# Linear attention and a routed expert network on one core: another order of work in a unit, the decay check beside the experts, one zero product a unit

## The chip, the cores and the metric

The kernel runs on one NeuronCore of a Trainium2 chip. Its engines are TensorE (PE in the rows; PEld is its weight load), VectorE (DVE), ScalarE (ACT), GpSimd (POOL) and SyncE (SP), which here only issues DMAs. Each engine works through its own instructions in order and waits on semaphores for the others. The metric is the device time of one execution in microseconds (us). Beside it stands one profiled execution, whose trace gives the start and the duration of every instruction.

## What is computed

Three stages, cut from the reference:

```python
for t in range(S):                       # gated linear attention, S=768, D=48, 4 batches x 8 heads
    state = alpha[:, :, t, :, None] * state + k[:, :, t] (x) v[:, :, t]
    y[:, :, t] = q[:, :, t] @ state
x = y as (3072 tokens, 384)
e = argmax(x @ w_gate)                   # one of 8 experts a token, gate g from the softmax
x = g * (relu(x @ w1[e]) @ w2[e])        # 384 -> 1024 -> 384
h = relu(x @ w_in)                       # 384 -> 2048
out = (h * h) @ w_out                    # 2048 -> 384
```

## The kernel before

*Units.* The attention is cut into 32 units: a unit is two heads of one batch and one half of the sequence, that is three chunks of 128 steps. Units 0 to 15 are the first halves, 16 to 31 the second halves, which begin from the state `smid` that the first half left. Channels of a unit lie on 112 partitions (48, a gap, 48). What is loaded for a unit is `qka`: q, k and alpha, 505 KB, in one of six buffers.

*A unit's work.* `scan` (L185, VectorE) gives A, the running product of alpha in each chunk. `prep_a` (L192 to L194, ScalarE) takes R = exp(-ln A), and in a third operation the decay check: Relu(alpha - 1), summed into `chk`, which shall be zero (`junk` is thrown away). `prep_p` (L203, L204) makes M = R k and R = A R on GpSimd, for the first two units on VectorE. `prep_k` and `prep_q` (L209, L214, VectorE) make `kk` = (2 - R) M and `qq` = q A. TensorE then takes `scores` = kk'qq into the bank `sct` (L229), `masked` (L236, VectorE) multiplies with the causal mask into `pt`, `ktr` (L245) transposes kk, and ScalarE copies it to `kn` (L246). `state_pe` (L256) makes the chunks' updates of the state in the bank `pst`; `state_0` to `state_4` carry the state over the chunks, with adds T on VectorE (L265) and multiplications by A on ScalarE (L261) in turn. `yout` (L293, L297) adds pt'v and S'qq into the bank `py`, ScalarE copies it to `yt`; `xout` (L316) multiplies with the identity and w_gate, which brings tokens on partitions and gives the logits, in `px`; ScalarE copies x (L318), VectorE adds the logits (L325, L327). All these buffers are rings of two to six.

*Zero products and warm-ups.* `fill` (L220) multiplies zeros into the bank that is to be overwritten, once ahead of the scores and once ahead of `yout` in every unit; `warm` (L102) does so ahead of the first units. They compute nothing.

*Routing.* Each four units make a group of tokens complete. `route_a` (seven operations on VectorE, L351 to L361), `route_b` (two products) and `route_s` (two operations) give each token its slot, and `scatter` (GpSimd's DMA, L388) writes the tokens to the slots in HBM. After unit 28 the first part of expert 0's tokens is loaded back (`xload(0)`, L404), and behind the loop it is transposed (L442) and the experts begin.

*Order.* All is in `tc.manual_schedule()`: the order of the calls in the code is the order on every engine. The loop's body handles several units at once: in pass u it works on the scores of u+1, the output of u and the logits of u-1, and prepares units further ahead. SP issues the loads in the same order and stops at each whose buffer isn't free.

*Experts.* For expert e a step f of eight does nine products of the first layer for 128 hidden channels (`gemm1`, L457, into the banks `pk` and `st` in turn), ScalarE's Relu (L470) and VectorE's remainder (L471), and nine products of the second layer for the step two before (L487). Beside it run the splits of the next weights into high and low parts (ScalarE L124, VectorE L125), the loads of weights (`wload`, L111, half an expert in a buffer of a ring of two), and the conversion of the last layers' weights from 64 bits (`conv`, L722 to L747, on SP, GpSimd, VectorE, ScalarE). The last stage (L778 to L830) does the same for the last network. `check` and `check_flag` sum `chk` and other conditions into a flag; where it isn't met, a general path runs, which isn't entered for this data.

## Time and profile before

| | us |
|---|---|
| median of three runs | 830.01 (829.81 to 835.50) |
| profiled execution, its own time | 824.76 |
| its span, first to last instruction | 822.8 |
| TensorE busy | 808.0 (98%) |
| VectorE busy | 554.6 (67%) |
| ScalarE busy | 394.7 (48%) |
| GpSimd busy | 273.7 (33%) |

The sums of busy time are means over stages that differ: the scan stage ends at some 164 us, the experts follow to some 420 us, then the last network. Idle time of an engine that is waited for by nobody costs nothing, so each stage is read by what ends its waits. Start-to-start distances say more of TensorE than durations do, since its products overlap.

### The profile page before, as it was taken

Reading aid. Unit: us, or ns where it says so; the run is one execution under the profiler, and the core shown is the slowest. Engines: PE = TensorE matmul, PEld = TensorE weight load, DVE = VectorE, ACT = ScalarE, POOL = GpSimd, SP = SyncE. Lnnn points to the kernel's source line nnn. Section 1 sums busy time; section 2 is a strip of 40 time slices with the busy share of each in tenths; the row PEclk is TensorE's granted clock in tenths of the full one; section 3 lists DMA queues with packets and bytes.
Section 4 is the critical chain, followed back from the end, with each engine's and each line's share of the span. In section 5 each row is a group of like instructions: output and inputs, shape, how many; then the busy total and the mean of one; then the engine's idle time right before and its main releaser. Section 6 shows DMA issues by size and latency. Waiting matters only on the chain.

```text
span 822.8 us, 14398 instructions
## 1 busy us (share of the span) xinstructions
PE 808.0 (98%) x5348; PEld 725.0 (88%) x5348; DVE 554.6 (67%) x1086; ACT 394.7 (48%) x885; POOL 273.7 (33%) x310
## 2 busy tenths in 40 slices
PE   8999999999999999999999999999999999999996
PEld 4777777799999999999989999988999999999996
DVE  6788988658588897865547878887464444344352
ACT  4777777545444545444344444444463233333342
POOL 2446766320165565510006566562000101011021
PEclk9899999999999999999999999999999999999999
DMA  9896892265767676754222443622412032021111
GB/s 270 267 293 195 256 270 81 54 222 159 246 197 215 221 248 186 228 199 136 72 86 83 114 142 105 212 61 68 154 60 96 19 97 82 35 96 58 40 59 62
DMA packets 56990, 118.12 MB, mean 144 GB/s; under 512 B 12272, under 2 KB 36688, under 8 KB 54608
## 3 DMA queue, kind: packets, MB, share of 16 engines
q1 hardware_dynamic: 52144, 100.59, 40.1%
q0 software_dynamic: 3072, 9.55, 3.1%
q10 hardware_dynamic: 1696, 6.98, 2.7%
q8 instruction: 44, 0.72, 0.4%
q14 instruction: 34, 0.28, 0.1%
HBM read 85.38 MB, written 31.73 MB: 142 GB/s over the span
## 4 chain that ended last, share of the span: by engine, by line
PE 88%; DVE 7%; issue 2%; ACT 2%; DMA 0%; POOL 0%; POOLq 0%; DVEq 0%; ACTq 0%
PE ph L457 38%; PE bp L797 10%; PE pair L487 10%; PE bpx L797 7%; PE bpy L797 7%; PE third L487 5%; PE sct L229 2%; PE px L316 2%; DVE pt L236 2%; PE py L293 2%; PE py L297 1%; DVE A L185 1%; PE pk L245 1%; PE sct L220 1%; PE pst L256 1%
## 5 line engine op out<-in xcount | busy, mean ns | idle before, releaser
L780 DVE TENSOR_TENSOR room<-room 128x512 f32<-128x512 f32 (+1 forms) x112 | 77.7, 694 | 147.3 <-ACT room L778 147.2
L778 ACT ACTIVATE room<-ph 128x512 f32<-128x512 f32 (+1 forms) x112 | 60.2, 538 | 235.8 <-PE ph L457 235.7
L457 PE MATMUL ph<-xth,w00h 128*128 128x512 f32 (+3 forms) x288 | 102.1, 354 | 0.0
L457 PE MATMUL ph<-xth,w00l 128*128 128x512 f32 (+3 forms) x288 | 100.8, 350 | 0.0
L457 PE MATMUL ph<-xtl,w00h 128*128 128x512 f32 (+3 forms) x288 | 100.2, 348 | 0.0
L830 POOL DMA_INDIRECT out<-room,id x24 | 23.6, 983 | 228.5 <-DVE room L813 223.3
L457 PE MATMUL ph<-xth,w10h 128*128 128x512 f32 (+2 forms) x264 | 95.6, 362 | 0.0
L457 PE MATMUL ph<-xtl,w10h 128*128 128x512 f32 (+2 forms) x264 | 95.4, 361 | 0.0
L457 PE MATMUL ph<-xth,w10l 128*128 128x512 f32 (+2 forms) x264 | 95.3, 361 | 0.0
L781 DVE TENSOR_TENSOR htl<-room,hth 128x512 fp32r<-128x512 f32 (+1 forms) x112 | 74.5, 665 | 15.2 <-ACT cvg L743 0.5
L727 POOL TENSOR_TENSOR cvg<-cvg,cvd 128x256 f32<-128x256 f32 x48 | 39.8, 829 | 120.5 <-issue 78.2
L732 POOL TENSOR_SCALAR cvc<-cvt 128x256 f32<-128x256 f32 x48 | 38.0, 792 | 103.1 <-DMA cvt<-wf 64.4
L470 ACT ACTIVATE hth<-ph 128x448 fp32r<-128x448 f32 (+2 forms) x72 | 36.2, 503 | 61.6 <-PE ph L457 59.4
L779 ACT ACTIVATE hth<-room 128x512 fp32r<-128x512 f32 (+1 forms) x112 | 63.9, 571 | 3.6
L471 DVE SCALAR_TENSOR_TENSOR htl<-ph,hth 128x448 fp32r<-128x448 f32 (+2 forms) x72 | 40.9, 568 | 30.1 <-ACT hth L470 29.6
L457 PEld LDWEIGHTS ph<-xtl,w00h 128*128 128x128 f32 x288 | 54.2, 188 | 6.7 <-DVE xtl L435 0.2
L457 PEld LDWEIGHTS ph<-xth,w00h 128*128 128x128 f32 x288 | 54.4, 189 | 5.1
L457 PEld LDWEIGHTS ph<-xth,w00l 128*128 128x128 f32 x288 | 54.2, 188 | 4.3
L457 PEld LDWEIGHTS ph<-xtl,w10h 128*128 128x128 f32 x264 | 49.5, 188 | 5.9
L457 PEld LDWEIGHTS ph<-xth,w10h 128*128 128x128 f32 x264 | 49.6, 188 | 4.6
L457 PEld LDWEIGHTS ph<-xth,w10l 128*128 128x128 f32 x264 | 49.6, 188 | 4.4
L203 POOL TENSOR_TENSOR M<-R,qka 112x384 f32<-112x384 f32 x30 | 29.9, 998 | 61.6 <-DVE pt L236 41.9
(218 smaller groups left out, 2109.2 us busy)
## 6 DMA issues: line engine op xcount, KB each, us to landing
wst<-wts SPq DMA_DIRECT2D x14, 1536.0 KB, 6.7
qka<-qka SPq DMA_DIRECT2D x30, 505.3 KB, 4.9
cvt<-wf SPq DMA_DIRECT2D x48, 256.0 KB, 4.0
xb<-x2t SPq DMA_DIRECT2D x10, 768.0 KB, 6.0
wf<-cvg SPq DMA_DIRECT2D x48, 128.0 KB, 3.0
xs<-zt SPq DMA_DIRECT2D x16, 343.9 KB, 7.2
x2t<-ot SPq DMA_DIRECT2D x8, 672.0 KB, 4.5
xr<-xs SPq DMA_DIRECT2D x7, 687.8 KB, 6.8
```

The costliest lines, as they stand in the source:

```text
L203: eng.tensor_tensor(M, R, c3(t[:, HS:2 * HS]), op=ALU.mult)
L457: nc.tensor.matmul(ph, a[:, o:o + 128], x[:, kc, :], start=(k == 0), stop=(k == 8))
L470: nc.scalar.activation(hi, ph, AF.Relu)
L471: nc.vector.scalar_tensor_tensor(lo, ph, 0.0, hi.bitcast(F32), op0=ALU.max, op1=ALU.subtract)
L487: nc.tensor.matmul(acc, a[:, ws], b, start=(f == 0 and i == 0), stop=(f == 7 and i == 2))
L727: nc.gpsimd.tensor_tensor(g, g, cvt.pop((k, "d")).bitcast(F32), op=ALU.mult)
L732: nc.gpsimd.tensor_scalar(c, cvt[k, "t"].bitcast(F32)[:, :, 1], F64_HI, -F64_HI, op0=ALU.min, op1=ALU.max)
L778: nc.scalar.activation(u, ph, AF.Relu)
L779: nc.scalar.activation(hi, u, AF.Square)
L780: nc.vector.tensor_tensor(g, u, u, op=ALU.mult)
L781: nc.vector.tensor_tensor(lo, g, hi.bitcast(F32), op=ALU.subtract)
L797: nc.tensor.matmul(acc, h[:, ts], w[:, ws], start=(f % 8 == 0 and k == 0), stop=(f % 8 == 7 and k == 2))
```

## The change

In the loop's body the calls stand in another order: the scan is that of unit u+3 and comes first (it was u+5 and came last); `masked(u + 1)` comes right behind the scores' first use; `prep_a` and `prep_p` are those of unit u+3 (were u+4), `prep_k` and `prep_q` come late; the logits' add comes behind `yout`. `M` has one buffer, not three. The decay check leaves `prep_a`: 32 loads of alpha (`dcheck`) and 32 Relus (`dcheck_act`) stand beside experts 1 to 6, two in three steps, in one buffer, and the flag is summed in expert 7. The zero product ahead of the scores is left out from unit 3 on. The first units' calls are rewritten, three warm-up products stand where seven stood, some copies go from VectorE to ScalarE, and the constants come in two loads.

```diff
-FILL = 1
+MB = 1
+FS, FY = 0, 1
+    cm = one.tile([128, C_N - C_K], F32, name="cm")
-                nc.sync.dma_start(ct, cst)
+                nc.sync.dma_start(ct, cst[:, 0:C_K])
+                nc.sync.dma_start(cm, cst[:, C_K:])
...
     def prep_a(u):
+        prep_ln(u)
+        prep_ex(u)
...
-        nc.scalar.activation(junk, t[:, 2 * HS:].rearrange("p (c s) -> p c s", s=CH + 1)[:, :, 1:], AF.Relu, bias=neg, accum_out=chk[:112, NU + u:NU + u + 1])
...
     def prep_p(u):
+        M = wk.tile([112, HC, CH], F32, tag="M", name="M", bufs=MB)
...
     def scores(u):
-        fill(sc[:, 0, 0:HS], FILL)
+        fill(sc[:, 0, 0:HS], FS if u > 2 else 1)
...
     def yout(u):
-        fill(py, FILL)
+        fill(py, FY if u > 2 else 1)
...
         for u in range(NU):
...
-            if u + 2 < NU:
-                prep_k(u + 2)
-                state_1(u)
-                prep_q(u + 2)
-            else:
-                state_1(u)
+            if u + 3 < NU:
+                scan(u + 3)
+            state_1(u)
             if u + 1 < NU:
                 scores(u + 1)
             state_2(u)
             if u + 1 < NU:
+                masked(u + 1)
                 ktr(u + 1)
-            state_3(u)
+            if u + 3 < NU:
+                prep_a(u + 3)
             g, gs = divmod(u - NP - 1, NP)
             if u > 0:
-                xout(u - 1)
-            if u + 1 < NU:
-                masked(u + 1)
-            if u + 4 < NU:
-                prep_a(u + 4)
+                xout_a(u - 1)
+            if u + 2 < NU:
+                prep_q(u + 2)
+            state_3(u)
+            if u + 2 < NU:
+                prep_k(u + 2)
+            if u + 3 < NU:
+                prep_p(u + 3)
             state_4(u)
-            if u + 4 < NU:
-                prep_p(u + 4)
             yout(u)
+            if u > 0:
+                xout_b(u - 1)
...
-            if u + 5 < NU:
-                scan(u + 5)
...
+    def dcheck(i):
+        t = orp.tile([112, HC, CH], F32, tag="dc", name="dc")
+        h, p = divmod(i, NPAIR)
+        nc.sync.dma_start(t, qka[h, p, :, 2 * HS:].rearrange("d (c s) -> d c s", c=HC)[:, :, 1:])
+        st["dc", i] = t
+    def dcheck_act(i):
+        t = st.pop(("dc", i))
+        nc.scalar.activation(t, t, AF.Relu, bias=neg, accum_out=chk[:112, NU + i:NU + i + 1])
...
+                c = e * 8 + f - 8
+                if c == -1:
+                    dcheck(0)
+                if 0 <= c < 48 and c % 3 < 2:
+                    i = c // 3 * 2 + c % 3
+                    dcheck_act(i)
+                    if i + 1 < NU:
+                        dcheck(i + 1)
-                if (e, f) == (2, 1):
+                if (e, f) == (7, 1):
                     check()
```

Three places show how the instructions move. The rows are the instructions of one engine in order, with the line, the operation, output and inputs and the size; lines of the changed kernel are some eight higher.

VectorE in the first units, before: from the first scan to the scan of unit 3.

```order
L185 SCALAR_TENSOR_TENSOR A<-qka,rst 112x387
L203 TENSOR_TENSOR M<-R,qka 112x384
L204 TENSOR_TENSOR R<-A,R 112x384
L209 SCALAR_TENSOR_TENSOR kk<-R,M 112x384
L214 TENSOR_TENSOR qq<-qka,A 112x384
L185 SCALAR_TENSOR_TENSOR A<-qka,rst 112x387 x2
L203 TENSOR_TENSOR M<-R,qka 112x384
L204 TENSOR_TENSOR R<-A,R 112x384
L236 TENSOR_TENSOR pt<-sct,ct 128x768
L209 SCALAR_TENSOR_TENSOR kk<-R,M 112x384
L214 TENSOR_TENSOR qq<-qka,A 112x384
L185 SCALAR_TENSOR_TENSOR A<-qka,rst 112x387
```

The same place in the changed kernel, to the scan of unit 3.

```order
L187 SCALAR_TENSOR_TENSOR A<-qka,rst 112x387 x2
L211 TENSOR_TENSOR M<-R,qka 112x384
L212 TENSOR_TENSOR R<-A,R 112x384
L217 SCALAR_TENSOR_TENSOR kk<-R,M 112x384
L222 TENSOR_TENSOR qq<-qka,A 112x384
L211 TENSOR_TENSOR M<-R,qka 112x384
L212 TENSOR_TENSOR R<-A,R 112x384
L244 TENSOR_TENSOR pt<-sct,cm 128x768
L187 SCALAR_TENSOR_TENSOR A<-qka,rst 112x387
L217 SCALAR_TENSOR_TENSOR kk<-R,M 112x384
L222 TENSOR_TENSOR qq<-qka,A 112x384
L187 SCALAR_TENSOR_TENSOR A<-qka,rst 112x387
```

The scan of unit 1 now stands ahead of unit 0's other work, and that of unit 2 behind the masking of unit 0.

VectorE in one unit of the loop's middle that doesn't route, before: from one scan to the next.

```order
L185 SCALAR_TENSOR_TENSOR A<-qka,rst 112x387
L209 SCALAR_TENSOR_TENSOR kk<-R,M 112x384
L265 TENSOR_TENSOR T<-pst,S 112x48
L214 TENSOR_TENSOR qq<-qka,A 112x384
L265 TENSOR_TENSOR T<-pst,S 112x48
L327 TENSOR_TENSOR x<-px,x 128x3x8
L236 TENSOR_TENSOR pt<-sct,ct 128x768
```

The same in the changed kernel, from its scan on.

```order
L187 SCALAR_TENSOR_TENSOR A<-qka,rst 112x387
L273 TENSOR_TENSOR T<-pst,S 112x48
L244 TENSOR_TENSOR pt<-sct,cm 128x768
L222 TENSOR_TENSOR qq<-qka,A 112x384
L273 TENSOR_TENSOR T<-pst,S 112x48
L217 SCALAR_TENSOR_TENSOR kk<-R,M 112x384
L335 TENSOR_TENSOR x<-px,x 128x3x8
```

The masking `pt` moved ahead of `qq` and `kk`, and `kk` from the unit's start to its end.

SP under the experts, before: from one store of tokens (x2t) to the next load of them (xr).

```order
L501 DMA x2t<-ot 128x3x448
L111 DMA wst<-wts 128x3072
L722 DMA cvt<-wf 128x512
L747 DMA wf<-cvg 128x256
L706 ISA
L706 DMA meta<-mt 112x4x2
L722 DMA cvt<-wf 128x512
L747 DMA wf<-cvg 128x256
L722 DMA cvt<-wf 128x512
L747 DMA wf<-cvg 128x256
L404 DMA xr<-xs 112x4x393
```

The same in the changed kernel, from the weight load on.

```order
L113 DMA wst<-wts 128x3072
L852 DMA dc<-qka 112x3x128
L710 ISA
L710 DMA meta<-mt 112x4x2
L726 DMA cvt<-wf 128x512
L751 DMA wf<-cvg 128x256
L852 DMA dc<-qka 112x3x128
L726 DMA cvt<-wf 128x512
L751 DMA wf<-cvg 128x256
L852 DMA dc<-qka 112x3x128
L412 DMA xr<-xs 112x4x393
```

The loads `dc` of the decay check stand between the others; each waits for ScalarE's use of the one before.

## Rows read from the trace of the kernel before

**Rows 1.** The page: span of the profiled execution and its instructions.

```profile
span 822.8 us, 14398 instructions
```

**Rows 2.** Windows: length, busy us of PE, PEld, DVE, ACT, POOL, PEclk, DMA, GB/s.

```profile
33.85:142.10 108.25, 106.86 (x1316) 84.60 (x1315) 96.10 (x223) 82.41 (x260) 65.82 (x64) 1.00 0.76 226
203.00:400.00 197.00, 197.00 (x1027) 183.79 (x1026) 148.97 (x277) 93.53 (x169) 77.40 (x97) 1.00 0.65 206
```

**Rows 3.** Timeline, TensorE, one unit: start us, us, operation [idle before].

```profile
42.23 0.44 PE L220 MATMUL sct<-zr 128*128 128x384 f32 x1
...
46.60 0.44 PE L220 MATMUL sct<-zr 128*128 128x384 f32 x1
46.97 0.94 PE L229 MATMUL sct<-qq,kk 48*128 48x128 f32 x12
...
49.92 0.64 PE L297 MATMUL py<-qq,S 48*48 48x128 f32 x8
...
50.50 0.55 PE L256 MATMUL pst<-v,kn 128*64 128x48 f32 x12
...
51.30 0.44 PE L220 MATMUL sct<-zr 128*128 128x384 f32 x1 [0.26 <-DVE pt L236]
```

**Rows 4.** VectorE by shape, 30 to 150 us: busy us, mean ns, idle before.

```profile
L236 DVE TENSOR_TENSOR pt<-sct,ct 128x768 f32<-128x768 f32 x27 | 25.6, 948 | 0.0
L214 DVE TENSOR_TENSOR qq<-qka,A 112x384 f32<-112x384 f32 x27 | 24.3, 900 | 0.0
L185 DVE TENSOR_TENSOR_SCAN A<-qka,rst 112x387 f32<-112x387 f32 x25 | 23.8, 950 | 0.0
```

**Rows 5.** Timeline: first routing operation, kk behind the seventh; qq beside R.

```profile
47.06 0.19 DVE L351 TENSOR_REDUCE rst<-x 128x3 f32<-128x24 f32 x1
...
48.50 0.55 DVE L209 SCALAR_TENSOR_TENSOR kk<-R,M 112x384 f32<-112x384 f32 x1
...
52.40 1.10 POOL L204 TENSOR_TENSOR R<-A,R 112x384 f32<-112x384 f32 x1
...
52.78 1.14 DVE L214 TENSOR_TENSOR qq<-qka,A 112x384 f32<-112x384 f32 x1
```

**Rows 6.** ScalarE by shape, 30 to 150 us: the decay check's two instructions.

```profile
L194 ACT ACTIVATE junk<-qka,neg 112x384 f32<-112x384 f32 x26 | 15.6, 600 | 0.0
...
L194 ACT ACTIVATION_READ_ACCUMULATOR junk<-qka,neg 112x1 f32 x26 | 4.8, 186 | 0.0
```

**Rows 7.** Timeline, first units: qq of unit 0, the scores of unit 4.

```profile
8.72 0.55 DVE L214 TENSOR_TENSOR qq<-qka,A 112x384 f32<-112x384 f32 x1
...
33.85 0.94 PE L229 MATMUL sct<-qq,kk 48*128 48x128 f32 x12
```

**Rows 8.** Windows in the first units, columns as in rows 2.

```profile
18.90:21.70 2.80, 1.30 (x20) 0.69 (x20) 2.80 (x7) 2.03 (x6) 1.53 (x3) 0.98 0.61 169
22.00:28.00 6.00, 6.00 (x39) 4.80 (x40) 3.81 (x8) 3.57 (x12) 2.08 (x3) 0.50 0.85 267
```

**Rows 9.** Timeline, last units: scores of unit 28, load of gathered tokens, first transpose.

```profile
142.10 0.94 PE L229 MATMUL sct<-qq,kk 48*128 48x128 f32 x12
...
153.29 0.32 SPq L404 DMA_DIRECT2D xr<-xs  x1
...
164.19 0.71 PE L442 MATMUL xt<-ct,xr 96*128 96x96 f32 x6
```

**Rows 10.** DMA issues by line: count, KB each, median us to landing.

```profile
wst<-wts SPq DMA_DIRECT2D x14, 1536.0 KB, 6.7
...
cvt<-wf SPq DMA_DIRECT2D x48, 256.0 KB, 4.0
```

**Rows 11.** Chain that ended last, one expert step: start us, us, what.

```profile
290.23 1.80 PE ph L457 x9
...
293.84 1.80 PE ph L457 x9
```

**Rows 12.** The page's groups: the experts' Relu on ScalarE.

```profile
L470 ACT ACTIVATE hth<-ph 128x448 fp32r<-128x448 f32 (+2 forms) x72 | 36.2, 503 | 61.6 <-PE ph L457 59.4
```

More of the change, by code (lines that the diff above doesn't have):

```diff
@@ L50 @@
 BLKS = (512, 512, 512, 512, 512, 256, 256)
[L52 to L53 removed]
+C_ID, C_WROW, C_LIM, C_EC, C_LOW, C_ROW, C_MASK, C_TRI = 0, 128, 152, 160, 168, 176, 200, 328
+C_K, C_N = 200, 456
 XW = DM + NE + 1
@@ L525, in main_path @@
         prep_a(0)
+        scan(1)
         prep_p(0)
@@ L528, in main_path @@
         prep_q(0)
-        scan(1)
         prep_a(1)
+        scores(0)
+        prep_p(1)
+        masked(0)
+        ktr(0)
         scan(2)
-        prep_p(1)
-        prep_a(2)
-        prep_p(2)
-        scores(0)
-        ktr(0)
-        warm(7, ps_1, "py", zt)
-        masked(0)
+        for x, r in enumerate((0, 64)):
+            nc.scalar.copy(wi[r:r + 48, :, x * 48:x * 48 + 48], ct[r:r + 48, r:r + 48].rearrange("p (a c) -> p a c", a=1).to_broadcast([48, NP, 48]))
+        warm(3, ps_1, "py", zt)
+        state_pe(0)
+        state_0(0)
+        prep_a(2)
         prep_k(1)
         prep_q(1)
-        scan(3)
-        prep_a(3)
-        prep_p(3)
-        state_pe(0)
-        state_0(0)
-        for x, r in enumerate((0, 64)):
-            nc.vector.tensor_copy(wi[r:r + 48, :, x * 48:x * 48 + 48], ct[r:r + 48, r:r + 48].rearrange("p (a c) -> p a c", a=1).to_broadcast([48, NP, 48]))
-        nc.vector.tensor_copy(tri, ct[:, C_TRI:C_TRI + 128])
-        nc.vector.tensor_copy(onr, ones)
-        nc.vector.tensor_copy(crow, ct[:, C_WROW:C_WROW + HC * NE])
-        nc.vector.memset(rone, 1.0)
-        nc.vector.memset(rone.rearrange("p (e i) -> p e i", e=NE)[:, :, 0:1], 0.0)
-        nc.vector.tensor_copy(ohx[0][:, :, 0], ct[:, C_EC:C_EC + 8])
-        scan(4)
+        prep_p(2)
         xsv = xs.rearrange("(e r) d -> e r d", e=NE)[:, 0:C].rearrange("e (p j) d -> e p j d", p=ZP)
@@ L603, in main_path @@
                     route_a(g)
+            if u == 1:
+                nc.scalar.copy(tri, cm[:, CH:CH + 128])
+                nc.scalar.copy(onr, ones)
+                nc.vector.tensor_copy(crow, ct[:, C_WROW:C_WROW + HC * NE])
+                nc.vector.memset(rone, 1.0)
+                nc.vector.memset(rone.rearrange("p (e i) -> p e i", e=NE)[:, :, 0:1], 0.0)
+                nc.vector.tensor_copy(ohx[0][:, :, 0], ct[:, C_EC:C_EC + 8])
             for k, x in enumerate(PRE):
```

28 lines of the change are left out of this document (13 added, 15 removed).

## The prediction

> **What bounds the kernel now.** I read the windows by stage first, then TensorE's instructions over one unit, then VectorE's and GpSimd's beside them. The profiled execution spans 822.8 us [rows 1]. From 203 us on, in the expert stage, TensorE is busy 197.00 us of 197.00 [rows 2]: nothing that the change does there can make the kernel faster, only slower. What can give time is the scan stage, units 0 to 31, up to the first transpose of the tokens at 164.19 us [rows 9]. Its middle, from the scores of unit 4 (33.85 us) to those of unit 28 (142.10 us), has TensorE busy for 106.86 of 108.25 us [rows 2], so it is TensorE that has to get shorter there too. VectorE is close behind with 96.10 us, 4.00 us for each of these 24 units; ScalarE has 82.41 (3.43 a unit), GpSimd 65.82 (2.74).
>
> One unit on TensorE [rows 3]: the zero product in front of the scores starts at 42.23 us and the next at 46.60, so a unit takes 4.37 us. The scores start 0.37 us behind their zero product (46.60 to 46.97), the products with the state 2.95 us behind the scores (49.92), the update of the state 3.53 us behind them (50.50). In the next unit the zero product shows an idle wait of 0.26 us until VectorE's masking `pt` is done (51.30): behind a unit that routes, VectorE is late. 24 units of 4.37 us are 104.9 us; the 3.4 us left of 108.25 belong to the six units in that stretch that route tokens.
>
> Why VectorE is late: the masking stands at the end of a unit's work, and the seven routing operations (47.06 until `kk` at 48.50 us, 1.44 us) stand ahead of the next unit's `kk` [rows 5]. Besides, `qq` takes 1.14 us where it starts 0.38 us after GpSimd's operation on R [rows 5]; its mean is 0.90 [rows 4], against 0.55 where it runs in unit 0, before GpSimd has such work [rows 7].
>
> **The change, part by part.** *Zero products.* 29 in front of the scores go, 24 of them between the scores of units 4 and 28. Each is worth 0.37 us if TensorE has its operands at once. Are they there? In the new order a unit on VectorE is scan, T, `pt`, `qq`, T, `kk`, logits. I set the start of the scores of unit u+1 at 0, and the period at 4.37 - 0.37 = 4.00. The scores end at 0.94 [rows 3], `pt` (0.95, [rows 4]) runs from 1.0 to 1.95, `qq` and `kk` (0.55 each) and one T behind them to about 3.2. The next scores need `kk` at 4.0: 0.8 us to spare. `M` has one buffer now, so GpSimd starts a unit's two operations only behind `kk`, at 3.2, and they run beside logits, scan, T and `pt`, not beside `qq` and `kk`; VectorE's 4.00 us a unit fall to at most 4.00 - (0.90 - 0.55) = 3.65. ScalarE loses the decay check's 0.60 + 0.19 us a unit [rows 6] and goes from 3.43 to 2.64. So TensorE stays the bound, unless the unit routes: then scan, T and `pt` stand behind 1.44 us of routing, `kk` is ready at 4.6 to 4.9, and the scores wait 0.25 us in the units of the first half, some 0.65 in the second half, where one T more waits for the update of the state. That is 6 x 0.45 = 2.7 us in place of the waits of 0.32 us (51.30 us less 0.5 behind the update at 50.50) that stand behind a routing unit now. I keep the 3.4 us of today and add 1.0: 24 x 4.00 + 3.4 + 1.0 = 100.4, against 108.25: **7.8 us**. Bounds: 9 us if nothing waits (24 x 0.37), 0 if VectorE's chain takes 4.37 again.
>
> *First units.* Unit 0's `qq` ends at 8.72 + 0.55 = 9.27 us [rows 7] in both kernels. Behind it VectorE now does M and R of unit 1 (shaped as `qq`: 1.2 us with the hand-over), `pt` 0, scan 2, `kk` 1, `qq` 1 (0.95 + 0.95 [rows 4] + 0.55 + 0.55, and hand-overs): the scores of unit 1 at 13.2 us. Then scan 3, T, `pt` 1, and `qq` 2 beside GpSimd (1.14), T, `kk` 2: the scores of unit 2 at 17.4. The copies of constants that stood here on VectorE are on ScalarE or behind unit 1. Unit 3 follows at 21.5, unit 4 at 25.8, against 33.85 [rows 7]: **8.0 us**. Where do they come from? Before, TensorE was busy for 1.30 us of the 2.80 from 18.9 to 21.7 us, and from 22 to 28 us its granted clock is 0.50, the 1.2 GHz level [rows 8]. Six us of work at half the clock hold 3 us that the full clock would not need; the other 5 are VectorE's two earlier scans and copies and the stall ahead of the slow stretch. In the new order I find gaps of 0.8 us at most on TensorE between 9 and 17 us, although four of seven warm-up products are gone, so I expect no such stretch. Bounds: 11 us if the loads and the hand-overs are quick, 3 us if the loads of the first units come late or the clock falls all the same.
>
> By the Trainium skill (TensorE: Matmul & The Clock Gate, "What's actually happening") the throttled clock is the default and only activity lifts it; zero products and warm-ups are such activity, so the rule speaks against taking them out. The trace agrees in [rows 8], where the low clock follows a stretch in which the engine was less than half busy. By the rule the risk is real and is a rival below.
>
> *Last units.* From the scores of unit 28 to the transposes are 22.09 us [rows 9]. The weight splits stay on VectorE there, and unit 28 still has a scan to do that was long done before, so I count only the four zero products: **1.5 us** (0 to 2.5). The load of the gathered tokens, issued at 153.29 us, 10.9 ahead of its use [rows 9], now comes behind M and R of unit 31 on GpSimd, some 3 us later; 8 us are left for 192 rows of 393 values, and 6.7 us are enough for 1,536 KB [rows 10], five times as much.
>
> *Scans three units ahead.* A unit's data is now wanted five units after its buffer came free rather than three, so loads have more room, not less. Nothing.
>
> *Decay check.* 32 loads of 168 KB and 32 x 0.79 us of ScalarE move under the experts. A step there is 3.61 us (290.23 to 293.84, [rows 11]), of which the first product of a pair of layers takes 1.80; its result must be read before that PSUM bank is written two steps later, 7.2 - 1.8 = 5.4 us, and the reading needs 1.2 of them (0.50 for the Relu [rows 12], about as much again for VectorE's part, and the hand-overs). So ScalarE may be some 4.2 us late. It is busy 93.53 us of 197 [rows 2], 1.7 us of a step; the check adds 0.79 in two steps of three. Each load is issued on SP when the one before it has been used, so a wait for its landing stands in ScalarE's order, ahead of the weight splits and of the next Relu, and on SP ahead of the weight and token loads. A 256 KB load lands 4.0 us after issue [rows 10]; where the next check comes a step later, ScalarE waits about half a us. **Nothing**, bounds 0 and -20 (below).
>
> *The rest.* The constants' load is cut in two, the check's sum comes in expert 7 rather than 2, in another bank: nothing waits for either within 20 us.
>
> **Sum.** 7.8 + 8.0 + 1.5 = 17.3 us off the profiled execution, whose span goes from 822.8 to about 805.5 and whose time from 824.76 to 807.5. The median of the three runs shown is 830.01 us, 5.2 above the profiled one, so I take the difference from the median: 812.7, and say **813**.
>
> **The rivals.** *VectorE or GpSimd keeps the period.* The single buffer of `M` closes a ring of `kk`, GpSimd's M and R (and a scatter, where there is one), and `kk`: 0.55 and GpSimd's 2.74 us a unit [rows 2], 3.3. If hand-overs and VectorE's own order stretch it to 4.37, the middle gives nothing: 830.0 - 9.5 = 820.5. For it: VectorE's 96.10 us already stand near the 108.25; against it: the 0.35 us of `qq` that go. Chance 0.14.
>
> *The clock falls.* One zero product a unit and three warm-ups don't hold it. A stretch as from 22 to 28 us costs 3 us; three of them in the start and behind routing units make 830.0 - 17.3 + 9 = 821.7. This is the result of the rule cited. Against it: with 4.00 us of work in 4.1 us TensorE's share stays above 95%. Chance 0.10.
>
> *The first units wait for data.* The start gives 3, not 8: 830.0 - 12.3 = 817.7. For it: the DMA share of 0.85 from 22 to 28 us [rows 8]. Chance 0.09.
>
> *Slower: ScalarE stuck at the decay check.* A check's load queues behind a weight load, which alone lands 6.7 us after its issue [rows 10]; ScalarE then waits, the Relu behind it is late, and TensorE stops. Between two Relus ScalarE has 1.7 + 0.8 us of its own work, so of the 4.2 us some 2.2 are free: a landing beyond 3.6 + 2.2 = 5.8 us costs its excess in the 16 pairs of checks that fall into neighbouring steps. From 5.8 + 17.3/16 = 6.9 us in each of them the whole gain is gone; at 8.0 the kernel takes 830.0 - 17.3 + 16 x 2.2 = 848. Against it: there are two weight loads for each expert, so most checks don't follow one. Chance 0.06 for a kernel slower than before by more than 1%.
>
> **Chances and range.** Forecast 0.61, with a range of its own from 806 to 818: the start between 5 and 11, the middle between 6 and 9, the end between 0 and 2.5. To 823 the range takes in the first three rivals; 805 is the start at its best with the middle at 9. About 1% (8.3 us) is what a measurement of this kernel can tell from no change. Faster by that: the forecast, the late data, half of the first two rivals, 0.82; within it the other halves, 0.12; slower 0.06.
>
> **What would show it.** Scores of unit 4 near 26 us and a granted clock of 1.00 from 10 us on: the start. Scores 4.0 us apart in units that don't route, `qq` and `kk` at 0.55 and M right behind `kk`: the middle. The first transpose near 147 us. TensorE at 100% in the expert stage with ScalarE's waits at the check under 2 us: the check is free. I am wrong if the scores stand 4.3 us apart or more, with `kk` or GpSimd's R ending last ahead of them; if the clock shows 0.50 behind 30 us; or if TensorE idles under the experts until a Relu that stands behind the check.

## The result and the profile after

The changed kernel takes 822.05 us (median of 17, 818.82 to 826.93), the kernel before 831.04 (17, 824.58 to 837.92): a ratio of 0.9906, interval 0.9880 to 0.9932. Here and below a ratio leaves out executions more than 1.5% above the fastest of their kernel; the medians have them in. That is a gain of 9 us where 17 were forecast. The two profiled executions differ by less, 822.8 us of span before and 820.3 after. The rest of the medians' difference fits executions of the kernel before that lose more to TensorE's granted clock: where the clock of each is on record, they took 821 to 825 us at a mean clock of 0.998 and 836 at 0.980. What follows compares the traces.

The page of the kernel after; the two rows under the heading are shares of the span, by engine and by line (before: TensorE 88%, DMA 0%):

```profile
span 820.3 us, 14361 instructions
...
## 4 chain that ended last, share of the span: by engine, by line
PE 73%; DMA 11%; DVE 7%; issue 3%; ACT 3%; POOL 1%; POOLq 0%; SPq 0%; ACTq 0%; DVEq 0%
PE ph L465 30%; PE bp L801 10%; PE bpx L801 7%; PE bpy L801 7%; DMA dc<-qka 5%; DMA wf<-cvg 5%; PE pair L495 4%; PE sct L237 2%; PE py L301 2%; PE px L324 2%; PE third L495 2%; PE py L305 2%; PE pst L264 1%; PE pk L253 1%; DVE htl L479 1%
```

Two kinds of transfer, the decay check's load (`dc`) and a transfer of the last weights' conversion (`wf`), now hold 10% of the chain. Windows of the kernel after, columns as in [rows 2]; the first is the middle (scores of unit 4 to those of unit 28), the second the last units, the third lies in the expert stage:

```profile
25.31:127.17 101.86, 98.36 (x1292) 80.12 (x1290) 84.74 (x221) 68.98 (x212) 60.68 (x63) 1.00 0.85 255
144.00:150.00 6.00, 5.17 (x45) 3.96 (x43) 2.31 (x9) 2.61 (x8) 2.68 (x3) 0.72 0.28 43
200.00:400.00 200.00, 192.28 (x978) 176.18 (x977) 140.38 (x270) 105.44 (x223) 73.80 (x98) 0.99 0.68 217
```

Against [rows 2] the middle is 6.4 us shorter, the last units run at a clock of 0.72, and TensorE, fully busy under the experts before, stands still for 7.7 of 200 us. One unit on TensorE, as [rows 3]: no zero product ahead of the scores (L237), and scores 4.00 us apart (the view ends within the second).

```profile
33.32 0.94 PE L237 MATMUL sct<-qq,kk 48*128 48x128 f32 x12
...
36.84 0.55 PE L264 MATMUL pst<-v,kn 128*64 128x48 f32 x12
37.32 0.38 PE L237 MATMUL sct<-qq,kk 48*128 48x128 f32 x2
```

The spans of ten profiled executions, cut at five instructions: the scores of unit 4, those of unit 28, the first transpose of gathered tokens, the first transpose of expert 1, and the first product of the last network's second layer. Times in us; "time" is the median.

| kernel | to unit 4 | middle | last units | expert 0 | experts 1 to 7 | rest | time (ratio to before) |
|---|---|---|---|---|---|---|---|
| before | 33.85 | 108.25 | 22.09 | 28.91 | 225.85 | 403.85 | 831.0 |
| after | 25.31 | 101.86 | 22.86 | 28.91 | 237.39 | 403.97 | 822.1 (0.991) |
| e1_none | 25.79 | 101.35 | 22.53 | 29.20 | 225.67 | 404.06 | 810.4 (0.976) |
| e5_scan | 25.48 | 109.31 | 22.49 | 28.91 | 225.63 | 403.58 | 818.0 (0.992) |
| e6_fs | 26.19 | 106.44 | 21.44 | 33.19 | 231.59 | 403.95 | 825.3 (0.995) |
| e8_keep | 25.76 | 99.70 | 21.31 | 28.88 | 238.93 | 403.92 | 820.6 (0.995) |
| e9_best | 25.23 | 99.73 | 21.32 | 31.74 | 225.31 | 404.67 | 811.2 (0.977) |
| e10_steps | 25.13 | 100.93 | 22.73 | 28.98 | 244.06 | 404.07 | 826.7 (0.997) |
| b1_check | 31.72 | 108.51 | 22.09 | 28.93 | 240.63 | 404.02 | 836.5 (1.014) |
| b2_fill | 29.21 | 102.55 | 24.95 | 28.85 | 225.72 | 403.92 | 824.2 (0.993) |

From before to after that is 8.5 us gained up to unit 4, 6.4 in the middle, 0.8 lost in the last units and 11.5 lost in experts 1 to 7: 2.5 in all. The ratios come from several groups of runs, each with its own executions of the kernel before. In the group of e5_scan, e8_keep, b1_check and e4_loads its median was 824.5 us, in that of the last two runs below 823.2, in the others 830 to 832. So compare ratios within a group, and stages across them.

The loss stands in two views. ScalarE and TensorE's waits from 195 to 405 us of the kernel after (us in total, times, longest):

```profile
ACT dc L857 <- DMA dc<-qka: 35.8, 13, 5.9
ACT cvg L747 <- DMA wf<-cvg: 23.0, 7, 7.0
...
PEld ph L465 <- DVE htl L479: 10.9, 9, 2.7
PE ph L465 <- DVE htl L479: 7.7, 8, 2.3
```

And SP's queue around one such wait, with ScalarE's Relu sum and the piece of the chain for the load:

```profile
235.59 0.38 SPq L113 DMA_DIRECT2D wst<-wts  x1
236.19 0.33 SPq L852 DMA_DIRECT2D dc<-qka  x1
...
237.13 0.53 SPq L751 DMA_DIRECT2D wf<-cvg  x1
245.82 0.33 SPq L852 DMA_DIRECT2D dc<-qka  x1
```

```profile
245.08 0.62 ACT L857 ACTIVATE dc<-dc,neg 112x384 f32<-112x384 f32 x1 [5.88 <-DMA dc<-qka]
```

```profile
232.31 3.06 DMA dc<-qka
236.19 8.80 DMA dc<-qka
```

A check's load issued 10.7 us behind a weight load (`wst`) lands after 3.06 us; issued 0.60 us behind one it takes 8.80. ScalarE stands for 5.88 us of them, with the next token and weight splits behind it, and SP issues nothing from 237.66 to 245.82 us.

TensorE's clock takes a part of the 11.5 us. Behind such a wait it is at its lower level, 0.50, for 3.4 us, whose half, 1.7 us, is my estimate of that part (windows as above):

```profile
278.00:282.60 4.60, 2.42 (x13) 1.93 (x11) 0.80 (x2) 2.09 (x6) 1.50 (x3) 1.00 0.04 5
282.60:286.00 3.40, 3.40 (x11) 3.00 (x10) 2.92 (x7) 1.62 (x4) 0.96 (x2) 0.50 0.59 166
```

### The profile page after: what moved, and what is told of

Same layout as the page of the kernel before. It is cut to its first block, busy times and chain, and to the rows that moved or that the text cites. A ratio compares the mean times of both kernels' runs of the same rounds, so it can differ in the third digit from the quotient of the medians.

```text
span 820.3 us, 14361 instructions
## 1 busy us (share of the span) xinstructions
PE 798.1 (97%) x5311; PEld 717.8 (88%) x5311; DVE 535.5 (65%) x1082; ACT 393.5 (48%) x889; POOL 263.5 (32%) x310
## 4 chain that ended last, share of the span: by engine, by line
PE 73%; DMA 11%; DVE 7%; issue 3%; ACT 3%; POOL 1%; POOLq 0%; SPq 0%; ACTq 0%; DVEq 0%
PE ph L465 30%; PE bp L801 10%; PE bpx L801 7%; PE bpy L801 7%; DMA dc<-qka 5%; DMA wf<-cvg 5%; PE pair L495 4%; PE sct L237 2%; PE py L301 2%; PE px L324 2%; PE third L495 2%; PE py L305 2%; PE pst L264 1%; PE pk L253 1%; DVE htl L479 1%
## 5 line engine op out<-in xcount | busy, mean ns | idle before, releaser
L736 POOL TENSOR_SCALAR cvc<-cvt 128x256 f32<-128x256 f32 x48 | 34.2, 712 | 104.8 <-DMA cvt<-wf 104.8
L211 POOL TENSOR_TENSOR M<-R,qka 112x384 f32<-112x384 f32 x30 | 29.9, 995 | 55.9 <-ACT R L201 34.8
```

Of the source, the lines that this page charges most:

```text
L211: eng.tensor_tensor(M, R, c3(t[:, HS:2 * HS]), op=ALU.mult)
L736: nc.gpsimd.tensor_scalar(c, cvt[k, "t"].bitcast(F32)[:, :, 1], F64_HI, -F64_HI, op0=ALU.min, op1=ALU.max)
```

## The experiments

**The check taken out.** Theory 1: the check's loads, with the waits for them, cost the 11.5 us. Rival: something else in the changed kernel does, or ScalarE's own work.

```diff
-                if c == -1:
-                    dcheck(0)
-                if 0 <= c < 48 and c % 3 < 2:
...
```

> The changed kernel without the decay check: the 32 loads of the decays under the experts and the 32 Relu sums are left out, everything else stands as in the changed kernel (so that check alone is missing from the computation). Theory 1 (the moved check costs the 11.6 us that the expert stage lost): first transpose near 150 us as before it, first product of the last network's second layer 254 to 256 us behind it, TensorE 100% busy from 205 us, time near 822.0 - 11.6 = 810.4 us (809 to 812). Theory 2 (the expert stage lost time to something else that the change brought: the conversion of the last weights, the order of the start of the experts, the clock): the stage stays near 266 us and the time near 822.

Measured: 810.44 us (three executions from 809.0 to 810.5, one of 822.7 at a mean clock of 0.980), ratio 0.9759 (0.9689 to 0.983); experts 1 to 7 in 225.67 us, as before the change. Then the work with one load left of 32:

```diff
-        t = st.pop(("dc", i))
+        t = st["dc", 0]
...
-                    if i + 1 < NU:
-                        dcheck(i + 1)
```

> The changed kernel with ScalarE's 32 Relu sums of the decay check where they are, but one load alone: all 32 work on the first pair's decays, so 31 loads are left out, and 31 pairs stay unchecked. Theory 1 (the loads and the waits for them cost the time, ScalarE's 0.79 us a check is covered): expert stage 254 to 256 us, time 810 to 812 us. Theory 2 (ScalarE's own work costs it: 32 x 0.79 = 25 us more on ScalarE, some of it on the path): the stage stays near 262 to 266 us, time 818 to 822 us.

Measured: 811.56 us, ratio 0.9772 (0.9716 to 0.9828); experts 1 to 7 in 225.62 us. And the loads with next to no work:

```diff
-        nc.scalar.activation(t, t, AF.Relu, ...)
+        nc.scalar.activation(t[:, :, 0:1], t[:, :, 0:1], AF.Relu, ...)
```

> The changed kernel with all 32 loads of the decay check, but Relu sums over the first of 128 columns only (3 values a row, about 0.2 us in place of 0.6; the other columns stay unchecked). If the loads and their waits cost the time: expert stage 264 to 267 us, ScalarE still waits about 30 us for the check's loads, time 819 to 823 us. If ScalarE's work on top of the waits is what tips it over: 254 to 260 us, time 811 to 815 us.

Measured: 819.02 us, ratio 0.9934 (0.9904 to 0.9964); experts 1 to 7 in 235.53 us, ScalarE waits 35.0 us at the check. The loads alone lose 9.7 us against the kernel before, with the clock at 1.00 throughout these experts; the kernel after loses 11.5, of which the clock is an estimated 1.7. So no part of ScalarE's own work shows. The size of the loss is not a fixed one: with the same loads in the same steps e6_fs loses 5.7 us and e8_keep 13.1 (table), so it probably hangs on how they fall among the other transfers. A stretch of the expert stage, without the check and with its work alone: TensorE is busy throughout, though ScalarE has 17 us more to do.

```profile
200.00:390.00 190.00, 190.00 (x987) 177.34 (x987) 143.82 (x271) 89.93 (x164) 78.01 (x98) 1.00 0.62 196
```

```profile
200.00:390.00 190.00, 190.00 (x987) 177.34 (x986) 143.22 (x271) 107.36 (x223) 75.00 (x97) 1.00 0.65 205
```

**The check alone, in the kernel before.** There only the check moves (its buffer is a token tile that is free by then):

```diff
-        nc.scalar.activation(junk, ..., AF.Relu, ...)   # in prep_a
...
+                    dcheck_act(i)                        # under the experts, as in the change
...
```

> The kernel before with one part of the change alone: the decay check moved under the experts, same loads, places and single buffer. Theory 1: the expert stage goes from 254.8 to 264 to 268 us; the scan stage may gain up to 2 us by the Relus that leave it; time 838 to 843 us, that is 8 to 12 us slower than before. Theory 2 (the loss needs the new order of the scan stage, its earlier experts or its clock): stage within 3 us of 254.8, time 827 to 832 us.

Measured: 836.47 us, ratio 1.0139 (1.0122 to 1.0156); experts 1 to 7 lose 14.8 us. This part alone makes the kernel slower; the loss needs nothing else of the change.

**Which wait: SP's or ScalarE's?** First three buffers and loads three ahead, on SP's queue as before:

```diff
+        g = ['dc', 'xth', 'xtl'][i % 3]     # two token tiles of expert 0 as further buffers
...
-                    if i + 1 < NU:
-                        dcheck(i + 1)
+                    if i + 3 < NU:
+                        dcheck(i + 3)
```

> The changed kernel with three buffers for the decay check and its loads issued three ahead of their use in place of one (the two further buffers are the token tiles of the first expert, free by then); same loads, same Relu sums. Theory 1a (what costs is the ring of one buffer: load, Relu, next load, with ScalarE and SP both waiting in it): no wait at the check above 1 us, expert stage back at 254 to 256 us, time 810 to 812 us. Theory 1b (the loads cost by taking the DMA engines from the weights and the conversion, or the Relu sums cost ScalarE's time): the waits move to the weights' or conversion's loads and the time stays at 818 to 823 us.

Measured: 814.95 us, ratio 0.9834 (0.9772 to 0.9897); experts 1 to 7 in 228.54 us; the time lies between the two forecasts. ScalarE waits at the check once from 195 to 405 us, for 2.8 us; 2.9 us against e1_none are left. Then one buffer, with the loads on ScalarE's queue:

```diff
-        nc.sync.dma_start(t, qka[...])
+        nc.scalar.dma_start(t, qka[...])
```

> The changed kernel with the decay check's loads issued on ScalarE's queue in place of SP's, still one buffer. SP then never waits for ScalarE at the check, and no weight or conversion load stands behind such a wait; ScalarE still waits for each landing. If the time is lost because SP is held up (conversion stores and loads late, ScalarE waiting for them): the waits for the conversion on ScalarE go, the stage falls to 256 to 259 us, time 812 to 816 us. If it is lost because a check's load lands late behind a weight load: a load that lands 7 to 9 us after its issue is still seen some 12 times, and the time stays at 818 to 823 us; if the landing was late only because both stood in SP's queue, the landing falls to about 3 us and the time to 810 to 813 us.

Measured: 837.54 us, ratio 1.0097 (1.0066 to 1.0128): the worst, experts 1 to 7 in 250.89 us, and beyond all three forecasts. SP is free, and ScalarE waits 54.4 us at the check. Why that is more than the 35.8 us with the loads on SP's queue no run separates. The trace shows why the other queue doesn't help (SP's weight load, then the check's load on ScalarE's queue and the Relu that waits for it):

```profile
346.45 0.33 SPq L113 DMA_DIRECT2D wst<-wts  x1
```

```profile
347.48 0.36 ACTq L852 DMA_DIRECT2D dc<-qka  x1
...
357.19 0.62 ACT L857 ACTIVATE dc<-dc,neg 112x384 f32<-112x384 f32 x1 [6.32 <-DMA dc<-qka]
```

Issued 1.03 us behind a weight load of the other queue, the load is there 9.7 us later. By the Trainium skill (DMA: Bandwidth & Descriptors, "Issuing engines are not separate DMA queues") DMAs run on the same 16 DMA engines whichever engine issued them; this trace agrees. Then the same loads in other steps of an expert, away from the two weight loads:

```diff
-                if 0 <= c < 48 and c % 3 < 2:
-                    i = c // 3 * 2 + c % 3
+                i = (e - 1) * 5 + (0, 0, 1, 2, 0, 0, 3, 4)[f]
+                if e > 0 and f in (0, 2, 3, 6, 7) and i < NU:
...
```

> The changed kernel with the decay check's 32 loads and Relu sums at other steps of the same experts, same one buffer, same SP queue: steps 0, 2, 3, 6 and 7 of each expert's eight, so that no check's load is issued within a step and a half behind one of the two weight loads (steps 0 and 4). If a check's load is late because a weight load of 1536 KB has all DMA engines (8 to 9 us from issue to use right behind one, 3 us elsewhere in the changed kernel): waits at the check fall from 35.8 to under 8 us in all, the expert stage from 266.3 to 255 to 258 us, time 811 to 814 us. If the ring of one buffer and SP's queue costs by itself, wherever the loads stand: waits of 20 us or more remain, stage 262 us or more, time 818 us or more.

Measured: 826.66 us, ratio 0.9970 (0.9932 to 1.0009); experts 1 to 7 in 244.06 us. In the trace one check's load is still 2.8 us behind a weight load and three are 3.4 to 4.6, where 12 were within 4.6 in the kernel after. The first expectation failed; of the second, stage and time came true, and waits of 20 us or more did not. The check's waits are halved, yet the stage is 6.7 us longer than in the kernel after. The clock has most of that: it is 0.50 for 6.8 us from 231.0 us on and again from 333.4 us on, by half an estimated 6.8 us against 1.7. The waits from 195 to 405 us:

```profile
ACT cvg L747 <- DMA wf<-cvg: 27.7, 5, 7.5
...
ACT dc L857 <- DMA dc<-qka: 17.0, 11, 3.5
```

```profile
220.76 0.44 SPq L113 DMA_DIRECT2D wst<-wts  x1
221.29 0.38 SPq L726 DMA_DIRECT2D cvt<-wf  x1
...
223.12 0.40 SPq L751 DMA_DIRECT2D wf<-cvg  x1
231.86 0.33 SPq L852 DMA_DIRECT2D dc<-qka  x1
```

```profile
221.77 8.53 DMA wf<-cvg
```

SP stands from 223.5 to 231.9 us at the check. What it issued in one burst before stands behind a weight load, and so the conversion's store, whose buffer ScalarE needs again, is on the chain with 8.53 us. So both halves have to be mended, and the last run of this question does that: loads on ScalarE's queue, three buffers, three ahead.

> The changed kernel with both: the check's loads on ScalarE's queue and three buffers with loads three ahead. With three buffers on SP's queue the expert stage took 257.7 us, 2.9 over that without a check. If these 2.9 us come from SP, which still waits for ScalarE at most of the checks' loads (96 us in 27): SP runs ahead as in the kernel before, stage 254 to 256 us, time 809 to 812 us. If they come from the loads' share of the DMA engines: stage 257 to 259 us with waits for the conversion's loads on ScalarE, time 812 to 816 us. If one buffer was not what made ScalarE's queue the worst place (stage 283.9 us): 265 us or more, time 820 us or more.

Measured: 811.9 us, ratio 0.9761 (0.9691 to 0.9831); experts 1 to 7 in 225.77 us (the stage that was forecast has expert 0 in it, whose clock is 0.50 for 10.2 us here and which takes 34.6). SP's waits at the check's loads with three buffers on its own queue, then a stretch of the expert stage, of e2_buf3 and of e11_actq3:

```profile
SPq L856 <- ACT dc L861: 96.4, 27, 6.9
```

```profile
200.00:390.00 190.00, 187.63 (x973) 174.45 (x972) 141.20 (x269) 105.95 (x220) 74.45 (x98) 1.00 0.72 226
```

```profile
200.00:390.00 190.00, 190.00 (x987) 177.16 (x986) 143.66 (x271) 109.89 (x225) 75.36 (x98) 1.00 0.74 229
```

The DMA engines are as busy (0.74 against 0.72), and TensorE does not wait: it is not the bandwidth that the check cost, but who stood still for its landing.

**What the check would cost in the scan stage.** It goes back to `prep_a`, in the new order:

```diff
+        a = st[u, "io"][:, 2 * HS:].rearrange(...)[:, :, 1:]
+        nc.scalar.activation(a, a, AF.Relu, bias=neg, accum_out=...)
...
```

> The changed kernel with the decay check back in the scan stage, as before the change: 32 Relu sums on the data that the units have loaded anyway, behind the two sums of R, and no loads for it under the experts. Theory 1 (the loads under the experts cost the 11.6 us): the expert stage (first transpose to the first product of the last network's second layer) takes 254 to 256 us. What ScalarE's 0.79 us a unit cost in the scan stage is open: ScalarE goes from about 2.6 to 3.4 us of a unit of 4.00 us. If that is covered, scores stay 4.00 us apart and the time is 810 to 812 us; if R comes late for it, scores go to 4.1 to 4.2 us and the time to 813 to 816 us. Theory 2 (the expert stage lost for another reason): 822 us or more.

Measured: 817.99 us, ratio 0.9921 (0.9904 to 0.9938), above both forecasts. The experts have their 225.63 us back, and the middle takes 109.31. Units that don't route are 4.00 us apart, those that route mostly 4.6 to 5.5. The chain that ended last runs through ScalarE there: of these 109.3 us ScalarE holds 51.3, VectorE 32.6 and TensorE 20.3, where in e8_keep (below) TensorE holds 85.9 of 99.7 and ScalarE nothing. A piece of it, with the check (L203), the copy of x (L328), the logits' add (L337) and the next unit's scan (L187):

```profile
60.10 0.60 ACT qka L203 x2
60.70 0.29 ACT x L328
...
61.01 0.18 DVE x L337
61.19 0.86 DVE A L187
```

VectorE's wait for that copy in the middle, with the check in the scan stage and in the kernel after:

```profile
DVE x L337 <- ACT x L328: 14.0, 18, 0.8
```

```profile
DVE x L335 <- ACT x L326: 3.1, 15, 0.3
```

The check stands in ScalarE's order between R and the copy. VectorE waits for the copy, the next scan comes late, and with it the next R. GpSimd, and so the single buffer of `M`, is not on that chain.

So the move did earn something where it came from: against e8_keep, whose middle holds no other wait, 9.6 us, of which the clock (0.98 in this middle) has an estimated 1.7. In the old order it earned nothing there: the middle of b1_check takes 108.51 us, that of the kernel before 108.25.

**The middle.** The zero product ahead of the scores put back into the new order, and taken out of the old one:

```diff
-FS, FY = 0, 1
+FS, FY = 1, 1
```

> The changed kernel with the zero product ahead of the scores back in units 3 to 31 (0.37 us each). If TensorE is what sets the period in the new order, as forecast: scores 4.37 us apart in units that don't route, 24 units from unit 4 to unit 28 take 108.5 to 110.7 us in place of 101.9, and the time is 829 to 831 us. If the new order has room on TensorE (VectorE or ScalarE set 4.00 us): scores stay 4.0 to 4.1 apart, time 822 to 824 us. The last units show whether the zero products hold the clock: 1.00 from 140 to 150 us in place of 0.76 to 0.82.

```diff
-        fill(sc[:, 0, 0:HS], FILL)
+        fill(sc[:, 0, 0:HS], FILL if u < 3 else 0)
```

> The kernel before with one part of the change alone: no zero product ahead of the scores in units 3 to 31. If the old order lets TensorE have the gain: scores 4.00 us apart in units that don't route, units 4 to 28 in 101 to 103 us (108.25 before), time 822 to 824 us. If VectorE's order (4.00 us of work a unit, masking last) holds the old period: 4.2 us or more apart, 105 us or more, time 827 us or more; then the new order is needed for the gain. If the clock falls below 1.00 in the middle without them, the rule of the clock is the reason.

Measured: 825.3 us, ratio 0.9951 (0.9919 to 0.9983), and 824.22, ratio 0.9927 (0.9884 to 0.9969). With the product back TensorE is the bound of the whole middle, and scores are 4.37 us apart as expected, though middle and time come out shorter than expected:

```profile
26.19:132.63 106.44, 106.44 (x1315) 84.61 (x1315) 84.93 (x220) 69.41 (x212) 60.01 (x63) 1.00 0.81 245
```

The old order without the product has scores 4.00 us apart and a middle of 102.55 us in its trace. So 5.7 us of the gain need no new order, and this one line alone has a ratio (0.9927) that can't be told from that of the whole change (0.9906). That execution, at 817.2 us, is the fastest of ten, and the other nine took 821 to 828 us at a mean clock of 0.980 to 0.992. Where their clock fell no trace shows.

Then unit 22, in which the scores of the kernel after are 5.83 us apart (99.45 to 105.28):

```profile
101.24 0.51 ACT L126 CAST w01h<-wst 128x384 fp32r<-128x384 f32 x1 [2.23 <-DMA wst<-wts]
...
101.79 0.56 DVE L127 TENSOR_TENSOR w01l<-wst,w01h 128x384 fp32r<-128x384 f32 x1 [2.56 <-ACT w01h L126]
102.19 0.74 PEld L324 LDWEIGHTS px<-wi,yt 112*128 112x128 f32 x6 [1.67 <-ACT yt L307]
102.19 0.80 PE L324 MATMUL px<-wi,yt 112*128 112x104 f32 x5 [1.46 <-ACT yt L307]
```

A split of expert 0's second weights waits for its load there, far from its place in the code (the first split of the second hand-ordered part, under the experts). A step's Relu written ahead of it keeps it back:

```diff
+            if f == 2:
+                g1a(0, f)
             while npre < min(16, 9 + f):
...
-            g1a(0, f)
+            if f > 2:
+                g1a(0, f)
```

> The changed kernel with one thing else: in the third step of the first expert the layer's products and Relu stand ahead of the weight split, not behind it. In the changed kernel the built program has that one split of expert 0's second weights far ahead of its place, in unit 22 of the scan stage, behind the load it needs, on ScalarE and VectorE; written behind a Relu it should stay among the experts. If ScalarE's wait of 2.23 us there costs the middle 1.8 us: the scores of units 22 and 23 stand 4.0 us apart in place of 5.83, scores of unit 28 at 125.4 us in place of 127.2, first transpose near 148.3, time 820.2 us if the experts keep that gain. If another work of unit 22 is late (routing, a scatter): the gap stays at 5.0 us or more.

Measured: 820.57 us, ratio 0.9954 (0.9936 to 0.9971); the scores of units 22 and 23 are 4.01 us apart, the middle takes 99.70. Experts 1 to 7 take 1.5 us more than in the kernel after.

**Better kernels, and the clock of the last units.** Both mended, the check moved on into the last network; and with four zero products back in the last units:

```diff
+            if 44 <= n < 108 and n % 2 == 0:
+                i = (n - 44) // 2
+                dcheck_act(i)
...
```

> The changed kernel with two things mended: the decay check (32 loads, three buffers, loads three ahead; 32 Relu sums) moved on into the last network, one check in every second of its steps 44 to 106, its flag read at the end; and the split of expert 0's weights kept among the experts as in the run before. In the last network one block's load of tokens (768 KB) comes every eight steps of 3.6 us and the conversion is over, so if loads under the experts cost because they share the DMA engines with weights and conversion, here nothing is lost: expert stage 254 to 256 us, last network 404 to 405 us, time 808 to 810 us. If TensorE in the last network hangs on ScalarE as it did under the experts: last network 408 us or more, time 813 us or more.

> The run before this (both mended) with the zero product ahead of the scores back in units 28 to 31 alone. TensorE is about 85% busy there and its clock fell to 0.76 and below between 144 and 150 us in the changed kernel's trace. If the four products keep it at 1.00: they cost at most 4 x 0.37 = 1.5 us and save the 1 to 5 us of slow stretch, time 1 to 3 us below the run before. If the clock falls all the same, or holds in both: 0.5 to 1.5 us above it.

Measured: 811.19 us, ratio 0.9772 (0.9726 to 0.9819), and 810.54, ratio 0.9763 (0.9719 to 0.9807): no difference between the two, and in both traces expert 0 takes 31.7 us in place of 28.9, at a lower clock. The products don't hold it. What goes with it is TensorE's wait behind the first transposes, for VectorE's `xtl`. Thirteen traces have the new order and no products in that wait. In five of them it is 1.77 to 1.90 us (e3_actq, e6_fs, e9_best, e9_bestz, e11_actq3), and in all five the clock falls within 5 us of the first transpose. In the other eight it is 0.48 to 0.65 us, and in none does it fall there; in six of these it fell ahead of the transposes, from 145.5 to 147.0 us on. What makes the wait longer was not looked for. The last two runs, on e11_actq3 with the split kept as in e8_keep, put products into that wait, and then into the gaps of units 30 and 31 too:

```diff
+        fill(xt0[:, 1, 0:HS], 5)
...
-        fill(py, FY if u > 2 else 1)
+        fill(py, 3 if u > 29 else 1)      # the second run only
```

> The changed kernel with the decay check's loads on ScalarE's queue, three buffers and three ahead, the weight split kept among the experts, and five zero products (0.16 us each at the full clock) into an unused half of the bank behind the first transposes, where TensorE waited 1.90 us for the first split of the tokens and where the granted clock stood at 0.50 from 152 to 160 us in the run without them. If that wait is what lets the clock fall: clock 1.00 from 150 us on, 28.9 to 29.2 us from the first transpose to the first transpose of expert 1 (31.7 to 35.2 in the runs whose clock fell), time 805 to 808 us. If the gaps of the last two units ahead of it let it fall: it falls all the same, time 809 to 812 us.

> The run before this with two more zero products ahead of the products with the state in units 30 and 31, where TensorE waits 0.3 to 0.65 us three times. If those gaps let the clock fall: clock 1.00 from 144 us on, time 0 to 3 us below the run before it. If they don't, the products cost at most 1.3 us.

Measured: 810.12 us (808.0 to 812.1), ratio 0.9841 (0.9818 to 0.9863), and 808.55 (808.4 to 811.7), ratio 0.9833 (0.9809 to 0.9856), in a group where the kernel before takes 823.2. The clock of the first run came as expected, its time (805 to 808 us were expected) did not. The window behind the first transposes, of e11_actq3 without and e12_fill2 with the products:

```profile
152.00:156.00 4.00, 4.00 (x20) 4.00 (x20) 1.90 (x10) 0.74 (x2) 0.00 (x0) 0.50 0.52 207
```

```profile
152.00:156.00 4.00, 4.00 (x37) 3.94 (x35) 3.59 (x12) 2.36 (x7) 1.64 (x2) 1.00 0.24 93
```

The clock stays at 1.00 there in both traces. Expert 0 takes 29.9 us, where the five traces in which the clock fell have 31.7 to 34.6. The 1.0 us above 28.9 is the longer wait itself, 1.71 us with the products in it; a cost of the products doesn't show. That they hold the clock rests on two traces against five: the same kernel without them was not run, and the eleven executions of the two runs, with a mean clock of 0.995 to 0.999, stand in a group in which the kernel before has 0.993 to 0.998 too. The second run's further products show nothing clear beyond that. Both are faster than the kernels before and after: none of the eleven took over 812.1 us, none of the kernel after under 818.8.

## Why the prediction was wrong, step by step

**The step that failed is the decay check, "Nothing, bounds 0 and -20".** It cost 11.5 us, two thirds of the forecast gain, and without it the forecast would have held: e1_none has a ratio of 0.976, where 812.7 to 830.0 is 0.979. In part that would have been luck: by the traces e1_none gains 14.2 us, and the medians have the clock that the kernel before loses on top. The rows were there. I priced the landing with the 4.0 us of a 256 KB load [rows 10], a median over loads that mostly don't follow a weight load, and put the collision aside because "most checks don't follow one". In the trace after, 9 of the 32 loads are issued within 3 us behind a weight load, and in part it is the check itself that brings them together: SP stands until ScalarE has used the buffer, then issues what has piled up in one burst, as with the weight loads at 190.86, 235.59 and 302.70 us, 1.0 to 3.3 us behind a check's load at which SP had stood. Four of the nine are on the chain with 7.83 to 8.80 us, beyond the 5.8 that I had set as the point from which it costs. And the rival named only the check's own load: the conversion's transfers `wf`, issued 0.9 to 1.0 us behind a weight load, are on the chain four times with 6.66 to 10.43 us. The price "nothing" also counted on two covers, SP's waiting and ScalarE's, as if each were free: e3_actq takes the first away and e2_buf3 the second, and they lose 25.2 and 2.9 us against e1_none's experts; e11_actq3 takes both and loses 0.1. The rival "ScalarE stuck at the decay check" was the right mechanism with a chance of 0.06; its price for a landing of 8.0 us in 16 pairs, 35 us, was too high: 9 loads, not 16, followed a weight load.

**The check's other end was missed too.** I gave the move from the scan stage no gain beyond room on ScalarE. In the new order it is worth up to 9.6 us there (e5_scan): on ScalarE the check stands ahead of the copy that VectorE waits for, and the next scan and R come late. That is VectorE's own order of the rival "VectorE or GpSimd keeps the period", not its ring of `M` and GpSimd, and it shows only with the check in place, and in units that route, not in all.

**Zero products and order: right.** Scores stand 4.00 us apart as forecast. `qq` and `kk` take 0.55 us each:

```profile
35.18 0.55 DVE L222 TENSOR_TENSOR qq<-qka,A 112x384 f32<-112x384 f32 x1
...
35.76 0.55 DVE L217 SCALAR_TENSOR_TENSOR kk<-R,M 112x384 f32<-112x384 f32 x1
```

The middle would give 8.55 us without the split in unit 22 (99.70), where 7.8 were forecast; of it the products are 6.7 (e6_fs against e8_keep: 0.37 us in 18 units, nothing in those that route) and the order 1.8. The order was not needed for the period of 4.00 us, which b2_fill has without it. The wait of the split took 1.8 to 2.2 of that back. Its wait is 0.25 us in the kernel before, and I had not looked at what else stands in a unit by then.

**First units: right in the sum, in part by luck.** The scores of units 1 to 4 start at 13.27, 17.30, 21.31 and 25.31 us; 13.2, 17.4, 21.5 and 25.8 were forecast. The slow stretch of [rows 8] is gone, as expected. But it belonged to that execution of the kernel before: in b1_check and b2_fill, with the old first units, the same window has a clock of 1.00 and unit 4 starts at 31.72 and 29.21 us (the second without the zero product from unit 3 on). Against these two the new first units gain 6.4 and 3.9 us, not the 8.5 of the trace.

**Last units: sign wrong.** 1.5 us were forecast, 0.8 lost. The scores of units 28 to 31 come 1.2 us closer together; then the clock falls (0.72 from 144 to 150 us). With the clock at 1.00 (e8_keep) the stretch is 0.8 us shorter, so half the term was right. This is the rival "the clock falls" at a place that I had not named: not in the middle, where the clock stays at 1.00 with TensorE busy 98.36 of 101.86 us, but in the last units, where from 142 to 146 us, just ahead of the fall, it is busy 3.14 of 4.00. It does not fall there in every execution: e8_keep, with the same products, keeps 1.00. By the Trainium skill (TensorE: Matmul & The Clock Gate, "What's actually happening") the full clock goes with how busy the engine has been recently; the last units of the trace after agree, and so do the traces of e12_fill and e12_fill2.

**Median against trace.** I carried the difference of the profiled execution to the median. It should have been clear from 824.76 beside 830.01 that most executions of the kernel before lose some 5 us to something that its trace does not show.

## What to carry to other kernels

A load that is issued only when its predecessor's buffer has been used makes two in-order engines wait for each other: price it by the landing behind the largest transfer of the stage, not by a median over loads that stand elsewhere, and give it buffers and a head start, on a queue that nothing else needs. Work taken off a half-idle engine can still be worth its full length if something that another engine waits for stands behind it in that engine's order. Run the parts of a change alone: one line here gave about as much as the whole. Read what a moved piece costs and earns at both its places before calling it free.

## What was not expected of the hardware

On the chain of the kernel after, the check's loads of 168 KB landed 2.6 to 3.1 us after their issue where that was more than 10 us behind a weight load of 1,536 KB, and 7.8 to 8.8 us where it was less than 3 us behind one. With the two on different queues, 9.7 us passed from a load's issue to its use (e3_actq). Waits of TensorE in a stage that was busy without a gap before cost clock as well as time: 3.4 us at 0.50 in the kernel after, twice 6.8 us in e10_steps. With the same program on the same chip, the mean granted clock of an execution lay between 0.980 and 0.998 in one group of runs (836 and 824 us) and between 0.993 and 0.998 in another some 35 minutes later.
